# Weight signs from a parametric ReLU, other banks for the first scan units, and an emptied table of due times

## The chip, the cores and the metric

The kernel runs on one core of a Trainium2 chip. A core has five engines with their own instruction queues: TensorE (matrix products, writing to the PSUM memory), VectorE, ScalarE and GpSimd (elementwise work), and SyncE, which here issues all the DMA transfers. Each engine works through its queue in order; semaphores make one wait for another. The metric is the device time of one execution in microseconds.

## The reference

A gated linear recurrence over four batch entries with eight heads gives a sequence of 768 positions per entry; its output, seen as 3072 tokens of 256 values, goes through two feed-forward blocks. Cut to what matters:

```python
def _attn_ref(x, a, B, C):            # x: (4, 8, 768, 32); a: (4, 8, 768); B, C: (4, 8, 768, 16)
    ...
    for c in range(nc):               # chunks of 32 positions
        la = log_a[:, :, sl]
        cum = np.cumsum(la, axis=-1)
        L = np.exp(cum[:, :, :, None] - cum[:, :, None, :]) * causal
        M = np.einsum('bhin,bhjn->bhij', Cc, Bc) * L
        y_intra = np.einsum('bhij,bhjd->bhid', M, xc)
        y_inter = np.einsum('bhin,bhnd->bhid', Cc, state) * np.exp(cum)[:, :, :, None]
        y[:, :, sl] = y_intra + y_inter
        state = decay_full[:, :, None, None] * state + np.sum(Bx, axis=2)

def _moe_ref(x, w_in, w_out):         # w_in: (256, 2048), w_out: (2048, 256)
    h = x @ w_in
    g = np.where(h > 0.0, h, np.exp(np.minimum(h, 0.0)) - 1.0)
    return g @ w_out

def _moe2_ref(x, w_a, w_b, w_out):    # w_a, w_b: (256, 1536), w_out: (1536, 256)
    return ((x @ w_a) * (x @ w_b)) @ w_out
```

The weights arrive as 64-bit floats; the other inputs as 32-bit floats.

## The kernel before, in words

**Tiles and stages.** The 3072 tokens form six tiles of 512. Stage A does the first feed-forward block tile by tile: a tile has eight pairs of 128-wide slices of the hidden layer. For each pair TensorE makes the up product into one of two PSUM buffers of two banks (`up0` for even pairs, `up1` for odd ones), ScalarE and VectorE make the activation, and TensorE accumulates the down product in the two banks `acc0` and `acc1`. Tile 0 uses whole 32-bit operands. Tiles 1 to 5 use operands split into a high and a low part (`hi_`, `lo_` for weights, `gh`, `gl` for activations), three matmuls for one product, twelve per slice. Stage B does the second block: two tiles at a time are taken as a 2 x 2 block product with seven products in place of eight, in 18 groups of two tiles.

**The scan.** The recurrence is cut into 24 units of 128 positions (six chunks of four batch entries). In a unit VectorE scans the decays of its heads (`scan`, L678, in two halves of four heads), TensorE makes the products of B and C (`cbm2` or `cbm`), VectorE multiplies the two (`mask`, L735), GpSimd weights `x` by the last column of the scan (`le`, then `xend`), TensorE makes the output and the addition to the state (`ym`, L770 and L774), and ScalarE copies both out (`state`, `x`). Four units feed one tile; units u0 to u3 feed tile 0. For these four the decays are spread over the partitions by TensorE (`spread`, L654) into two PSUM banks, not loaded by DMA as for the later units. The first pair of tile 0 needs the output of u0 and u1 for its first half of columns, the second pair, in `up1`, that of u2 and u3.

**Weights.** Each weight tile holds 1024 columns as pairs of 32-bit words (`raw`, or `fx` for early ones). `scale` (L523) multiplies the top word, read as a 32-bit float, by 2^-112; `shift` (L528) moves it left by three bits, which drops the sign; `sign` (L531) puts the sign back; `last3` turns the low word into the last three bits; `put` adds them. The result is `m`. Of 17 tiles, eight are made before or in tile 0 (weights of the first block, named m_99, m_100, ... in the listings, in this order: w_in 0, w_out 0, w_in 1, and so on), nine later, for stage B.

**What sets the order.** The whole program is a list of steps with an engine or a choice of two, an estimated cost, the steps it depends on, and a due time. A planner (`Plan.emit`) imitates the engines: it takes, of all ready steps, the one that could start in the earliest window of 0.25 us, and among these the one due first. That fixes each engine's order. `MOVE` shifts the due times of single steps. Where TensorE would wait in the first 50 us by the planner's reckoning, it puts in matmuls on a tile of zeros (`warm`, L419). `Buf.take` gives the steps that must be done before a buffer is written again; `tied` joins two buffers that lie in one PSUM tile.

## Time and profile before

| | |
|---|---|
| time before, median of 3 runs | 616.45 us (616.45 to 617.79) |
| the profiled execution, its own time | 616.54 us |
| its span, first to last instruction | 614.5 us |
| TensorE busy, share of the span | 607.7 us, 99% |
| VectorE busy | 395.9 us, 64% |
| ScalarE busy | 372.1 us, 61% |
| GpSimd busy | 332.0 us, 54% |

Busy time is the sum over an engine's instructions without overlaps. Matmuls are pipelined, so a busy TensorE need not be working on useful products: the zero matmuls count as busy as well. A matmul on 32-bit operands shows as two records in the trace. Idle time is put down to the event that ended it.

### The profile page before, as it was taken

What the parts mean: (1) busy time and instruction counts of PE and PEld (TensorE: products, weight loads), DVE (VectorE), ACT (ScalarE), POOL (GpSimd) and SP (SyncE); (2) the same over time, 40 slices, a digit from 0 to 9 for tenths busy, and PEclk for the clock granted to TensorE, in tenths of its full rate; (3) what the DMA queues carried; (4) which work ended last, traced back from release to release, by engine and by line L of the source; (5) the groups of instructions that cost most, each with busy time, mean ns of one, the idle gap of its engine ahead of it and who ended that gap; (6) DMA issues with size and microseconds to landing.
All of it is one profiled execution on the core that took longest, in us unless ns stands there. A gap on an engine that the chain in (4) does not pass through costs nothing.

```text
span 614.5 us, 9444 instructions
## 1 busy us (share of the span) xinstructions
PE 607.7 (99%) x3627; PEld 481.8 (78%) x3627; DVE 395.9 (64%) x534; ACT 372.1 (61%) x529; POOL 332.0 (54%) x250
## 2 busy tenths in 40 slices
PE   9999999999999999999999999999999999999997
PEld 8875457778778877877888888888888888888885
DVE  7878869788787878868655646756533446433344
ACT  2565767756767766647767655556544556545453
POOL 2423466565556564256445476767655656555542
PEclk9999999999999999999999999999999999999999
DMA  8949633677677736410000000000100000100001
GB/s 236 313 164 306 200 102 126 224 243 248 195 239 271 285 120 201 157 52 0 2 1 1 1 0 1 0 1 1 69 0 2 0 1 0 70 0 1 1 0 68
DMA packets 33404, 59.94 MB, mean 98 GB/s; under 512 B 2736, under 2 KB 13904, under 8 KB 33360
## 3 DMA queue, kind: packets, MB, share of 16 engines
q1 hardware_dynamic: 33360, 59.35, 29.0%
q8 instruction: 28, 0.46, 0.3%
q14 instruction: 16, 0.13, 0.1%
HBM read 47.61 MB, written 11.73 MB: 97 GB/s over the span
## 4 chain that ended last, share of the span: by engine, by line
PE 98%; DVE 0%; ACT 0%; issue 0%; POOL 0%; POOLq 0%
PE acc L857 6%; PE acc L853 6%; PE up L841 6%; PE up L842 6%; PE acc L854 6%; PE up L844 6%; PE up L1186 5%; PE up L1182 5%; PE up L1183 5%; PE up L832 5%; PE acc L832 5%; PE acc L1242 4%; PE acc L1244 4%; PE acc L1243 4%; PE cbank L1242 3%; PE cbank L1244 3%
## 5 line engine op out<-in xcount | busy, mean ns | idle before, releaser
L1271 DVE TENSOR_TENSOR x<-x 128x512 f32<-128x512 f32 x36 | 30.6, 854 | 67.4 <-POOL x L1315 67.0
L940 ACT ACTIVATE e<-up 128x1024 f32<-128x1024 f32 x44 | 45.1, 1026 | 38.5 <-PE up L844 26.2
L1277 POOL TENSOR_TENSOR gl<-x,gh 128x512 fp32r<-128x512 f32 x35 | 48.5, 1387 | 35.4 <-ACT gh L1274 35.2
L961 POOL TENSOR_TENSOR gl<-e,gh 128x1024 fp32r<-128x1024 f32 x20 | 50.9, 2543 | 27.2 <-ACT gh L954 21.9
L1315 POOL TENSOR_TENSOR x<-e,x 128x512 f32<-128x512 f32 x36 | 46.7, 1314 | 33.7 <-ACT e L1254 32.9
L853 PE MATMUL acc<-gh,hi_w_out 128*128 128x512 f32 x160 | 63.6, 397 | 0.0
L854 PE MATMUL acc<-gh,lo_w_out 128*128 128x512 f32 x160 | 62.4, 390 | 0.0
L944 ACT ACTIVATE e<-e,bias 128x1024 f32<-128x1024 f32 x44 | 50.8, 1154 | 0.9
L857 PE MATMUL acc<-gl,hi_w_out 128*128 128x512 f32 x160 | 51.3, 396 | 0.0
L678 DVE TENSOR_TENSOR_SCAN ab<-ab,delta 128x512 f32<-128x512 f32 x36 | 50.0, 1406 | 2.0 <-DMA ab<-a_seg 2.0
L541 POOL TENSOR_TENSOR m<-m,raw 128x1024 int32<-128x1024 int32 x11 | 26.7, 2430 | 25.8 <-DVE m L531 5.5
L841 PE MATMUL up<-xh,hi_w_in 128*128 128x512 f32 x96 | 39.4, 410 | 0.0
L950 DVE SCALAR_TENSOR_TENSOR up<-e,up 128x512 f32<-128x512 f32 x40 | 27.7, 693 | 17.8 <-ACT e L944 17.1
L842 PE MATMUL up<-xh,lo_w_in 128*128 128x512 f32 x96 | 37.5, 390 | 0.0
L1183 PE MATMUL up<-gh,lo_w_out 128*128 128x512 f32 x96 | 37.4, 389 | 0.0
L1182 PE MATMUL up<-gh,hi_w_out 128*128 128x512 f32 x96 | 37.4, 389 | 0.0
L1262 DVE TENSOR_TENSOR p<-acc,p 128x512 f32<-128x512 f32 x36 | 24.2, 688 | 20.3 <-PE acc L1244 18.2
L950 DVE SCALAR_TENSOR_TENSOR e<-e,up 128x512 f32<-128x512 f32 x48 | 30.6, 678 | 10.4 <-ACT e L944 10.4
L1274 ACT CAST gh<-x 128x512 fp32r<-128x512 f32 x36 | 22.4, 624 | 23.6 <-DVE x L1271 23.5
L1262 DVE TENSOR_TENSOR x<-acc,x 128x512 f32<-128x512 f32 x36 | 23.9, 686 | 19.3 <-PE acc L1244 19.2
L1277 POOL TENSOR_TENSOR gl<-p,gh 128x512 fp32r<-128x512 f32 x18 | 23.9, 1325 | 21.2 <-issue 21.2
L853 PEld LDWEIGHTS acc<-gh,hi_w_out 128*128 128x128 f32 x160 | 30.1, 188 | 6.0
(306 smaller groups left out, 1733.1 us busy)
## 6 DMA issues: line engine op xcount, KB each, us to landing
ab<-a_seg SPq DMA_DIRECT2D x18, 512.0 KB
parts<-raw SPq DMA_DIRECT2D x64, 128.0 KB
sm<-parts SPq DMA_DIRECT2D x16, 512.0 KB
p<-in_xb SPq DMA_DIRECT2D x20, 256.0 KB
raw<-in_w_out SPq DMA_DIRECT2D x4, 1024.0 KB
fx<-in_w_out SPq DMA_DIRECT2D x3, 1024.0 KB
out_t<-m SPq DMA_DIRECT2D x12, 256.0 KB
raw<-in_w_in SPq DMA_DIRECT2D x2, 1024.0 KB
```

What stands on the lines that cost most here:

```text
L832: nc.tensor.matmul(ps, w_mm(name, wm, f, c), src, start=start, stop=stop)
L841: nc.tensor.matmul(ps, w_mm(name, whi, f, c), xh[:, c, :], start=(c == 0), stop=False)
L842: nc.tensor.matmul(ps, w_mm(name, wlo, f, c), xh[:, c, :], start=False, stop=False)
L853: nc.tensor.matmul(accs[m], w_mm(name, whi, f, m), gh, start=(f == 0), stop=False)
L854: nc.tensor.matmul(accs[m], w_mm(name, wlo, f, m), gh, start=False, stop=False)
L857: nc.tensor.matmul(accs[m], w_mm(name, whi, f, m), gl, start=False, stop=(f == last))
L944: nc.scalar.activation(gf, gf, AF.Identity, bias=bias[:, 0:1])
L950: nc.vector.scalar_tensor_tensor(u[:, k, :] if on_dve else gf[:, k, :], gf[:, k, :], 0.0, u[:, k, :], op0=ALU.min, op1=ALU.max)
L961: nc.gpsimd.tensor_sub(gl.ap, gf, gh.ap.bitcast(F32))
L1182: nc.tensor.matmul(a4[m].ap, w_mm("w_out2", whi, f, m), gh, start=first, stop=False)
L1183: nc.tensor.matmul(a4[m].ap, w_mm("w_out2", wlo, f, m), gh, start=False, stop=False)
L1277: eng[e].tensor_sub(tap("l" + w), tap(wa), tap("h" + w).bitcast(F32))
```

## The change

**Sign.** `scale` becomes a ScalarE activation, a parametric ReLU with scale 2^-112 and slope 2^32 for negative values. A negative weight so gets 32 added to its exponent, and this bit becomes the sign bit in the shift. `sign` and its step are gone; `put` waits for `shift` instead. `scale` has ScalarE alone now, where it had a choice of ScalarE and VectorE.

**Banks.** u0 to u3 all spread their decays into `acc0` and `acc1`; before, u2 and u3 used the two banks of `up1`. Their products of B and C go to `cbank` and one bank of `up0` (u0, u2), one bank each of `up0` and `up1` (u1), and both banks of `up1` (u3). Banks of one PSUM tile no longer wait for each other (`tied` is gone). The last column `le` of u0 to u3 is copied by ScalarE, no longer by VectorE.

**Planner.** The transfer model allows eight loads in flight at a time and has other constants; the engines' hand-over costs are smaller; zero matmuls are put in for a wait less 0.2 us; `MOVE` is empty. The set-up of the head mask is a step of its own.

The diff, cut to its core:

```diff
-MM = 0.2282
+MM = 0.2272
...
 MOVE = {
-    ("bc", (0, 1, 1)): {"": 7.7, "cast": 5.0},
-    ("bc", (0, 2, 0)): {"": -5.4, "load": 2.3, "rest": -6.3},
...
 }
...
     def take(self):
         old, self.users = self.users, []
-        for b in self.tied:
-            old = old + b.users
         return old
...
-    SYNC = {"PE": 0.27, "ACT": 0.12, "DVE": 0.12, "POOL": 0.12, "SP": 0.0}
-    SAME = {"PE": 0.0, "ACT": 0.06, "DVE": 0.1, "POOL": 0.08, "SP": 0.0}
+    SYNC = {"PE": 0.27, "ACT": 0.12, "DVE": 0.12, "POOL": 0.12, "SP": 0.05}
+    SAME = {"PE": 0.0, "ACT": 0.04, "DVE": 0.06, "POOL": 0.04, "SP": 0.0}
+    LAG = {"PE": 0.0, "ACT": 0.1, "DVE": 0.08, "POOL": 0.04}
...
-                    m = int((start - free["PE"]) * rate / 0.054)
+                    m = int((start - free["PE"] - 0.2) * rate / 0.054)
...
                 for kb in c:
-                    dma = max(dma, end + 1.75) + kb / 250.0
-                    end += 0.45
-                free[e], end = end, dma + 0.6
+                    if len(landed) >= 8:
+                        end = max(end, landed[-8])
+                    dma = max(dma, end + 1.5) + kb / 310.0 + 0.05
+                    landed.append(dma)
+                    end += 0.46
+                free[e], end = end, dma
...
-                free[e] = end
+                free[e] = end - self.LAG[e]
...
-    for i in range(2):
-        cb1[1 + 2 * i].tied, cb1[2 + 2 * i].tied = [cb1[2 + 2 * i]], [cb1[1 + 2 * i]]
...
         def scale(e):
-            if e == "ACT":
-                nc.scalar.mul(m, top.bitcast(F32), 2.0 ** -112)
-            else:
-                nc.vector.tensor_scalar(m, top.bitcast(F32), 2.0 ** -112, None, op0=ALU.mult)
+            nc.scalar.activation(m, top.bitcast(F32), AF.Prelu, scale=2.0 ** -112, alpha=2.0 ** 32)
...
-        def sign(e):
-            nc.vector.scalar_tensor_tensor(mi, top, -0x80000000, mi, op0=ALU.bitwise_and, op1=ALU.bitwise_or)
...
-        i2 = add({"ACT": 1.155, "DVE": 0.75}, scale, i1, mbf.take(), due=due, port=True)
-        i3 = add({"DVE": 0.75}, shift, i2, due=due, port=True)
-        i4 = add({"DVE": 1.3}, sign, i3, due=due, port=True)
+        i2 = add({"ACT": 1.155}, scale, i1, mbf.take(), due=due, port=True)
+        i3 = add({"DVE": 0.7}, shift, i2, due=due, port=True)
...
-            sp = accb if u < 2 else cb1[3:5]
-            cb_ = [[cbb, cb1[1]], [cb1[2], cb1[3]], [cbb, accb[1]], [cbb, cb1[3]]][u]
+            sp = accb
+            cb_ = [[cbb, cb1[1]], [cb1[2], cb1[3]], [cbb, cb1[1]], [cb1[3], cb1[4]]][u]
...
-            i_le = add({"DVE": 0.1} if n == 0 else {"ACT": 0.2}, last_col, i_scan, le.take(), due=due)
+            i_le = add({"ACT": 0.2}, last_col, i_scan, le.take(), due=due)
```

**What moves.** In the listings a number behind a name tells copies of a buffer apart: sm_79 and sm_80 hold B and C of u0 and u1, and of u2 and u3; ab_81, ab_82, f_hi_w_out_94 and f_lo_w_out_95 are the decays of u0 to u3; up_117 and up_118 are `up0` and `up1`.

TensorE, from u1's output (L770, L774) to u2's products of B and C (L719), before:

```order
L770 MATMUL ybank<-ab_82,p_78 32x128 x8
L774 MATMUL ybank<-xe,p_78 32x64 x4
L654 MATMUL up_118<-a_114,delta 128x128 x8
L719 MATMUL cbank<-sm_80 128x128
L719 MATMUL acc_120<-sm_80 128x128
```

TensorE, from u1's output (L667, L671) to u3's products of B and C (L616), in the changed kernel:

```order
L667 MATMUL ybank<-ab_82,p_78 32x128 x8
L671 MATMUL ybank<-xe,p_78 32x64 x4
L551 MATMUL acc_119<-a_114,delta 128x128 x4
L551 MATMUL acc_120<-a_114,delta 128x128 x4
L616 MATMUL up_118<-sm_80 128x128 x8
```

Behind u1's output the spread of u3 follows now, into the accumulator banks; the spread of u2 (L551) and its products stand in the ten rows ahead of it. Between u1's products and its output 42 zero matmuls stood before; there are none now.

VectorE, from the shift of weight m_99 to u3's masks, before:

```order
L528 TENSOR_SCALAR m_99<-m_99 128x1024
L531 SCALAR_TENSOR_TENSOR m_99<-raw_75,m_99 128x1024
L678 SCALAR_TENSOR_TENSOR f_hi_w_out_94<-up_118,delta 128x512 x2
L695 COPY le_67<-f_hi_w_out_94 128x8
L735 TENSOR_TENSOR f_hi_w_out_94<-cbank,f_hi_w_out_94 128x512
L735 TENSOR_TENSOR f_hi_w_out_94<-acc_120,f_hi_w_out_94 128x512
L678 SCALAR_TENSOR_TENSOR f_lo_w_out_95<-up_118,delta 128x512 x2
L695 COPY le_68<-f_lo_w_out_95 128x8
L528 TENSOR_SCALAR m_100<-m_100 128x1024
L531 SCALAR_TENSOR_TENSOR m_100<-fx_92,m_100 128x1024
L735 TENSOR_TENSOR f_lo_w_out_95<-cbank,f_lo_w_out_95 128x512
L735 TENSOR_TENSOR f_lo_w_out_95<-up_118,f_lo_w_out_95 128x512
```

VectorE, the same place in the changed kernel:

```order
L430 TENSOR_SCALAR m_99<-m_99 128x1024
L575 SCALAR_TENSOR_TENSOR f_hi_w_out_94<-acc_119,delta 128x512
L575 SCALAR_TENSOR_TENSOR f_hi_w_out_94<-acc_120,delta 128x512
L575 SCALAR_TENSOR_TENSOR f_lo_w_out_95<-acc_119,delta 128x512
L632 TENSOR_TENSOR f_hi_w_out_94<-cbank,f_hi_w_out_94 128x512
L632 TENSOR_TENSOR f_hi_w_out_94<-up_117,f_hi_w_out_94 128x512
L575 SCALAR_TENSOR_TENSOR f_lo_w_out_95<-acc_120,delta 128x512
L430 TENSOR_SCALAR m_100<-m_100 128x1024
L632 TENSOR_TENSOR f_lo_w_out_95<-up_118,f_lo_w_out_95 128x512 x2
```

Both `sign` (L531) and both `le` (L695) are gone, the shift of m_99 stands directly ahead of u2's scan, and the two halves of u3's scan lie on both sides of u2's masks.

ScalarE, from its first weight operation to u1's copies, before:

```order
L523 ACTIVATE m_99<-raw_75 128x1024
L788 COPY state<-ybank 128x64
L806 COPY x_90<-ybank 128x2x128
L536 ACTIVATE raw_75<-raw_75 128x1024
L788 COPY state<-ybank 128x64
L806 COPY x_90<-ybank 128x2x128
```

ScalarE, the same place in the changed kernel:

```order
L590 COPY le_67<-ab_81 128x8
L427 ACTIVATE m_99<-raw_75 128x1024
L434 ACTIVATE raw_75<-raw_75 128x1024
L685 COPY state<-ybank 128x64
L703 COPY x_90<-ybank 128x2x128
L590 COPY le_68<-ab_82 128x8
```

The last columns of u0 and u1 (L590) are new here, and both weight operations (L427, L434) stand ahead of u0's state and x now.

VectorE, the first odd pair of tile 1, from its activation (L950) on, before:

```order
L950 SCALAR_TENSOR_TENSOR up_118<-e_84,up_118 128x512 x2
L959 TENSOR_TENSOR gl_89<-up_118,gh_86 128x512 x2
L485 TENSOR_TENSOR lo_w_out_944<-m_104,hi_w_out_862 128x1024
L950 SCALAR_TENSOR_TENSOR e_83<-e_83,up_117 128x512 x2
```

VectorE, the first odd pair of tile 1, from its activation (L847) to its residual (L856), in the changed kernel:

```order
L847 SCALAR_TENSOR_TENSOR up_118<-e_84,up_118 128x512 x2
L388 TENSOR_TENSOR lo_w_out_809<-m_102,hi_w_out_740 128x1024
L388 TENSOR_TENSOR lo_w_out_822<-m_104,hi_w_out_796 128x1024
L632 TENSOR_TENSOR ab_81<-cbank,ab_81 128x512
L856 TENSOR_TENSOR gl_89<-up_118,gh_86 128x512 x2
```

Two low parts of weights and a mask now stand between the activation and the residual of this pair; nothing did before.

## Rows read from the trace of the kernel before

**Rows 1.** Busy time by stretch: start, end, length, each engine, clock, DMA.
```profile
core 0: us, PE busy (x) PEld busy (x) DVE busy (x) ACT busy (x) POOL busy (x), PEclk, DMA share, GB/s
0.00:31.00 31.00, 28.63 (x378) 26.11 (x379) 25.44 (x38) 12.90 (x19) 10.28 (x18) 1.00 0.90 275
31.00:600.00 569.00, 569.00 (x3208) 447.71 (x3207) 364.01 (x488) 354.99 (x503) 317.88 (x229) 1.00 0.26 89
400.00:500.00 100.00, 100.00 (x443) 82.81 (x442) 47.33 (x64) 54.65 (x97) 60.64 (x45) 1.00 0.03 11
```

**Rows 2.** Timeline of TensorE to 31 us: start, length, instruction, count, idle before.
```profile
1.06 3.22 PE L419 MATMUL ybank<-zt 128*128 128x128 bf16 x31 [1.06 <-POOL zt L415]
...
18.73 2.05 PE L654 MATMUL up<-a,delta 128*128 128x128 f32 x16 [0.51 <-DVE f_hi_w_out L678]
...
21.40 1.99 PE L832 MATMUL up<-x,m 128*128 128x256 f32 x8
...
27.51 0.64 PE L770 MATMUL ybank<-f_lo_w_out,f_lo_w_out 128*32 128x128 f32 x16
...
29.07 1.50 PE L419 MATMUL ybank<-zt 128*128 128x128 bf16 x24 [0.81 <-ACT x L806]
...
30.41 1.95 PE L832 MATMUL up<-x,m 128*128 128x256 f32 x8
```

**Rows 3.** Chain that ended last, in order of time: start, length, instructions.
```profile
10.10 1.09 PE up L719 x16
...
30.57 1.78 PE up L832 x8
```

**Rows 4.** Timeline of VectorE, units u0 to u3.
```profile
5.26 2.34 DVE L678 TENSOR_TENSOR_SCAN ab<-acc,delta 128x512 f32<-128x512 f32 x2 [0.28 <-PE acc L654]
...
11.76 1.29 DVE L735 TENSOR_TENSOR ab<-up,ab 128x512 f32<-128x512 f32 x2
12.97 0.68 DVE L528 TENSOR_SCALAR m<-m 128x1024 int32<-128x1024 int32 x1
13.68 1.22 DVE L531 SCALAR_TENSOR_TENSOR m<-raw,m 128x1024 int32<-128x1024 int32 x1
16.34 2.34 DVE L678 TENSOR_TENSOR_SCAN f_hi_w_out<-up,delta 128x512 f32<-128x512 f32 x2 [1.43 <-PE up L654]
...
20.82 2.34 DVE L678 TENSOR_TENSOR_SCAN f_lo_w_out<-up,delta 128x512 f32<-128x512 f32 x2 [0.47 <-PE up L654]
```

**Rows 5.** Timeline of ScalarE to 30 us.
```profile
0.80 1.28 ACT L423 ACT_TABLE_LOAD   x1 [0.80 <-PEq L1487]
...
9.23 1.18 ACT L523 ACTIVATE m<-raw 128x1024 f32<-128x1024 f32 x1 [6.93 <-DMA raw<-in_w_in]
...
17.64 1.13 ACT L523 ACTIVATE m<-fx 128x1024 f32<-128x1024 f32 x1 [2.76 <-DMA fx<-in_w_out]
...
28.65 0.37 ACT L806 COPY x<-ybank 128x256 f32<-128x256 f32 x1
```

**Rows 6.** Instructions by line and shape: count, busy us, mean ns, idle before.
```profile
L944 ACT ACTIVATE e<-e,bias 128x1024 f32<-128x1024 f32 x44 | 50.8, 1154 | 0.9
...
L940 ACT ACTIVATE e<-up 128x1024 f32<-128x1024 f32 x44 | 45.1, 1026 | 38.5 <-PE up L844 26.2 <-PE up L832 7.9 <-POOL p L756 1.7
...
L950 DVE SCALAR_TENSOR_TENSOR up<-e,up 128x512 f32<-128x512 f32 x40 | 27.7, 693 | 17.8 <-ACT e L944 17.1
...
L959 DVE TENSOR_TENSOR gl<-up,gh 128x512 fp32r<-128x512 f32 x40 | 25.7, 683 | 7.5 <-ACT gh L954 7.5
...
L954 ACT CAST gh<-up 128x1024 fp32r<-128x1024 f32 x20 | 20.3, 1014 | 12.8 <-DVE up L950 12.7
...
L531 DVE SCALAR_TENSOR_TENSOR m<-raw,m 128x1024 int32<-128x1024 int32 x12 | 14.6, 1219 | 0.1
...
L419 PE MATMUL ybank<-zt 128*128 128x128 bf16 x135 | 9.9, 237 | 1.9 <-POOL zt L415 1.1 <-ACT x L806 0.8
```

**Rows 7.** Waits of SyncE's queue to 90 us: total, times, longest.
```profile
SPq L514 <- POOL m L541: 4.3, 1, 4.3
```

More of the change, by code (lines that the diff above doesn't have):

```diff
@@ L64 @@
-    ("group", 4): {"": 0.8, "hi": -2.2, "lo": 1.7, "mm3": 2.5},
-    ("group", 5): {"": -8.2, "cp": 0.2, "dn_h": 0.5},
-    ("late", 0): {"comb": 2.6},
-    ("late", 1): {"": 0.1},
-    ("late", 3): {"": -10.3},
-    ("late", 4): {"high": 3.0},
-    ("late", 5): {"": 3.5, "high": 9.5},
-    ("late", 6): {"": 8.5, "high": -13.9},
-    ("late", 7): {"": -14.4, "comb": 10.6},
-    ("late", 8): {"": 0.3, "high": -6.8},
-    ("pair", (0, 0)): {"": -7.7},
-    ("pair", (0, 5)): {"": -2.6},
-    ("pair", (0, 7)): {"": 2.8},
@@ L100 @@
-    ("pair", (5, 0)): {"": 5.7},
-    ("pair", (5, 1)): {"up_a": -3.1},
-    ("pair", (5, 3)): {"up_a": -7.0},
-    ("pair", (5, 4)): {"up_a": 0.1},
-    ("pair", (5, 5)): {"": 5.8},
-    ("pair", (5, 6)): {"": 4.7, "up_a": -6.5},
-    ("pair", (5, 7)): {"": -0.7, "dn_h": 3.4},
-    ("split", ("w_in", 0)): {"high": -20, "rest": -2.9},
-    ("split", ("w_in", 1)): {"": -1.8, "high": -2.8},
-    ("split", ("w_in", 3)): {"": 6.1, "high": 3.2},
-    ("split", ("w_out", 0)): {"": 1.5},
-    ("split", ("w_out", 1)): {"": -8.2},
@@ L112 @@
-    ("unit", 0): {"": 8.5, "ld0": -15.4, "ld_x": -9.9, "mask": -5.0},
-    ("unit", 1): {"ld0": 7.0, "ld_x": 13.0},
-    ("unit", 10): {"ld_a": -20, "st_bd": -5.0},
-    ("unit", 11): {"scan": 6.0, "st_up": 8.5},
-    ("unit", 12): {"": -12.6, "ld_a": 5.9},
-    ("unit", 13): {"": -7.7, "<lambda>": 3.6, "scan": -4.3},
-    ("unit", 14): {"": -0.6, "ld_sm": 4.0, "scan": -2.6, "st_bd": -4.2},
-    ("unit", 15): {"": -3.8, "<lambda>": 11.8, "cbm": 6.9, "ld_a": 18.7, "scan": 5.9},
-    ("unit", 16): {"": -8.1, "st_bd": -7.0},
@@ L121 @@
-    ("unit", 17): {"": -9.6, "last_col": 17.8},
-    ("unit", 18): {"scan": 6.9, "st_bd": 10.0},
-    ("unit", 19): {"": 6.4, "cbm": 8.3, "st_bd": -16.1},
-    ("unit", 2): {"ld0": 12.2},
-    ("unit", 20): {"": -4.8, "<lambda>": -18.3, "ld_db": -6.6, "ld_x": -2.5, "scan": 9.0},
-    ("unit", 21): {"": 5.1, "ld_x": -4.6, "mask": 8.5, "scan": -4.0},
-    ("unit", 22): {"<lambda>": 14.0, "cbm": -2.1, "ld_a": -9.9, "scan": 1.5, "x_lo": 15.3},
-    ("unit", 23): {"mask": 7.9, "scan": 4.2, "st_bd": -12.9},
@@ L129 @@
-    ("unit", 3): {"ld_x": 12.1},
-    ("unit", 5): {"last_col": 16.9, "x_hi": 20},
-    ("unit", 6): {"": 2.8, "<lambda>": 6.4, "ld_a": -5.0, "ld_x": 2.7},
-    ("unit", 7): {"": 3.0, "<lambda>": -1.2, "ld_a": -1.9, "ld_x": -3.6, "st_bd": -0.4},
-    ("unit", 8): {"": 10.9, "ld_a": -7.3, "scan": -4.6, "st_up": 6.9, "x_lo": 3.9, "xend": -3.1},
-    ("unit", 9): {"": 2.0, "ld_a": -3.0, "ld_sm": 2.5},
-    ("w", ("w_in", 1)): {"shift": -19.7},
-    ("w", ("w_in", 2)): {"put": 8.6},
-    ("w", ("w_in", 3)): {"": 4.1, "scale": 7.8},
@@ L138 @@
-    ("w", ("w_out", 1)): {"put": -20, "sign": -11.6},
-    ("w", ("w_out", 2)): {"sign": -6.5},
-    ("w", ("w_out", 3)): {"load": -16.2, "sign": 4.2},
-    ("wb", ("w_a", 0)): {"": -0.2, "last3": 7.5, "load": 0.2},
-    ("wb", ("w_a", 1)): {"": -11.5},
-    ("wb", ("w_a", 2)): {"": 12.0, "shift": -2.6, "sign": -2.6},
-    ("wb", ("w_b", 0)): {"": -8.4, "scale": -20, "sign": -6.0},
-    ("wb", ("w_b", 1)): {"": -8.8, "last3": 18.2, "shift": 18.2},
-    ("wb", ("w_b", 2)): {"": 10.0, "last3": -3.0, "load": 7.0, "sign": 15.3},
@@ L147 @@
-    ("wb", ("w_out2", 0)): {"": 4.1, "sign": -9.5},
-    ("wb", ("w_out2", 1)): {"sign": 6.5},
-    ("wb", ("w_out2", 2)): {"last3": 13.0, "load": 16.4, "put": 10.3, "scale": 12.6, "shift": -0.1, "sign": -3.4},
-    ("xset", 1): {"": -11.8, "x_h": -13.3, "x_l": 0.9},
 }
@@ L214, in emit @@
         port, dma, done = 0.0, 0.0, 0
+        landed = []
         self.log = []
@@ L753, in st_bd @@
                     hmask.rearrange("p (q e) -> p q e", e=2).unsqueeze(3).to_broadcast([P, 4, 2, D]))
-            i_sbd = add({"POOL": 0.82}, st_bd, i_state[b], sbd.take(), i_ones, due=due, port=True)
+            i_sbd = add({"POOL": 0.82}, st_bd, i_state[b], sbd.take(), i_heads, due=due, port=True)
             i_cd = add({"POOL": 0.72}, lambda e: nc.gpsimd.tensor_mul(cd, cd, dbt), i_p, i_db, due=due, port=True)
```

45 lines of the change are left out of this document (8 added, 37 removed), and 4 rows, old and new, of the table MOVE.

## The prediction

> **What bounds the kernel now.** I read the busy times by stretch first [rows 1]. From 31 to 600 us TensorE is busy for 569.00 of 569.00 us at a granted clock of 1.00, which is the 2.4 GHz level; no other engine passes two thirds there (VectorE 364 us, ScalarE 355 us). Nothing that the change takes off VectorE can shorten that stretch. In the first 31 us TensorE counts 28.63 us as busy, but its timeline [rows 2] shows that part of this is padding: L419, a matmul on a tile of zeros, which runs 135 times in all [rows 6], 31 of them at the very start and 24 just ahead of 30.41. Its real waits are small, 1.06, 0.51 and 0.81 us [rows 2], because the padding stands where waits would be. So time can be won only in front of the second pair of tile 0, the last work that has padding ahead of it; it starts at 30.41 [rows 2]. The VectorE timeline [rows 4] shows what that start waits for: one chain of scan, mask, scan, mask over the units u0 to u3, with the preparation of the first weights in between.
>
> **The change, part by part.**
>
> *Sign.* Per weight tile of 1024 columns one VectorE instruction of 1219 ns goes [rows 6], 17 of them (twelve in that row, five on the early buffers), some 21 us. In the saturated stretch this is worth nothing, since TensorE covers it. In the first 31 us one sign (1.22 us, at 13.68 [rows 4]) stands directly ahead of u2's scan and a second one ahead of u3's masks; these two are on the chain. On ScalarE the multiplication of weight m0 (1.18 us [rows 5]) becomes a parametric ReLU of the same shape, and the one weight of 17 that VectorE scaled goes there too. The trace has no such ReLU: the nearest rows are ScalarE's exponential (1026 ns) and its identity with a bias (1154 ns) on as many columns [rows 6]. I take 1.15 us, no change; at the other bound, twice that, the first weight holds u0's state and u1's last column 1.15 us longer, all of it on the chain. A second function table is not loaded: the trace has one table load, 1.28 us at 0.80 [rows 5], and the changed order has one too.
>
> *Banks.* Before, u2 and u3 spread their decays into the two banks of `up1`, and u3's spread had to wait for u2's scan; VectorE sat idle 1.43 us at 16.34 and 0.47 us at 20.82 for these two spreads [rows 4]. Now all four units use the two accumulator banks, and u2's spread stands on TensorE ahead of u1's output matmuls instead of behind them (listing on TensorE). It needs only u1's scan, so it is done by about 12.9, before VectorE asks for it.
>
> *Last column.* The copy `le` of u0 to u3 leaves VectorE for ScalarE. For u1 it queues there behind both operations of weight m0 and the copies of u0 (listing on ScalarE), which start when the weight lands, at 9.23 [rows 5]: 9.23 + 1.18 + 1.13 for the second operation, of the same shape, + about 0.5 for the copies gives 12.05. Before, u1's masks started at 11.76 [rows 4]; I charge the change 0.35 us.
>
> *Walk through the start.* TensorE has 19 zero matmuls first, not 31; at 3.22/31 = 0.104 us [rows 2] that is 1.25 us less, but u0's scan gains only the 0.28 us that it waited [rows 4]. Then on VectorE: u1's masks 12.1 to 13.4 (1.29), one shift (0.68) to 14.05, u2's scan (2.34) to 16.4, where it ended at 18.7. Next come half of u3's scan, u2's masks, the other half, one shift and u3's masks (listing on VectorE): 1.2 + 1.3 + 1.2 + 0.7 + 1.3 = 5.7, so 22.05. Needed on the way is weight m1, whose load landed by 17.64 [rows 5]; its two ScalarE operations end at 19.9, ahead of the shift at 20.1. On TensorE: u2's output 19.0 to 19.7; the first pair of tile 0, whose two halves stand together now, 2 x 1.78 [rows 3] to 23.25; u3's output to 24.0. ScalarE does the first exponential (1.03), then u3's copies, to 24.9; before, the copy of `x` ended at 28.65 + 0.37 = 29.02 [rows 5]. Fifteen zero matmuls at 1.50/24 = 0.0625 us [rows 2] make 0.95: the second pair starts at 25.9. Against 30.41 that is **4.5 us earlier**. The work left behind this point is the same in both kernels, and TensorE had no wait in it [rows 1].
>
> *Loads.* SyncE issues in order. The load of the third w_in tile now stands ahead of u5's decays and its rows of B and C. It waits for GpSimd to finish with weight m1, as it did before (4.3 us [rows 7]), and now u5's loads wait behind it, until about 24 by the walk. u5's scan follows u4's masks, which come after the second pair and the first down matmuls, near 35; the loads have some 5 us of cover. Without it, u5's masks and its output on TensorE would be late by as much.
>
> *Emptied table.* Due times decide between steps that are ready together; they shift the interleaving in the saturated stretch. The tightest place I find is the odd pairs of tiles 1 to 5: VectorE makes their residual out of a bank of `up1`, and the pair after next needs this bank. The chain is 1.03 + 1.15 + 2 x 0.69 + 1.01 + 2 x 0.68 = 5.9 us [rows 6], and TensorE does three groups of 12 matmuls meanwhile, 36 x 100/443 = 8.1 us [rows 1], which leaves 2.2 us less hand-overs. What else VectorE does between the last two steps eats this: in all 20 odd pairs 27 instructions before, 31 after, at most three in one pair in either kernel (second listing on VectorE: the first pair, one of the worst). The stalls that this could cause were absent before. I take 0 for it, and 0.4 us per odd pair as the other bound.
>
> **Sum.** The profiled execution took 616.54 us, 614.5 of it span and 2.0 around it, 0.09 above the median of 616.45. 616.5 - 4.5 = **612.0 us**.
>
> **The rivals.**
>
> *A, the forecast:* 610.5 to 613.5. For it: each piece gained is a wait or an instruction in rows 2 and 4 that has no place in the new order.
>
> *B, the start is gained in part.* Weight operations stand at the head of ScalarE's and VectorE's queues more often now. A load that lands 2 us later, or a ReLU 1.15 us slower, goes through to the masks. Price 1 to 4 us: 613 to 616.
>
> *C, the odd pairs stall (slower).* If the residuals come late by 0.4 us beyond the room in each of 20 odd pairs, and the first group stage loses 2 us to the same cause, that is 10 us: 612 + 10 = 622. It decides against the change from 0.32 us per pair (6.4 us in all). Against it: the new order alternates up and down matmuls strictly, pair by pair, which the old one did not, and 31 instructions are hardly more than 27.
>
> *D, the clock at the start.* 94 of the 135 zero matmuls are gone. The trace shows 0.104 us for each of the first 31 and 0.0625 for the last 24 [rows 2], near the ratio of 1.2 to 2.4 GHz, although the granted clock reads 1.00 in the whole stretch [rows 1]; the later rows all hold the faster pace. If with fewer zero matmuls TensorE ran at the lower level from 5 to 19 us, three spreads of 2.0 [rows 2], four score groups of 1.1 [rows 3] and two outputs of about 0.7, 11.8 us, would take 23.6: 12 us later, less 2 us of slack, less the 4.5 gained: 616.5 + 5.5 = 622. The Trainium skill, "TensorE: Matmul & The Clock Gate", Part 1 ("The HAM clock gate"), says that the throttled state is the default and that activity releases it; the first row agrees, and by that rule alone the padding was no waste. Against D: in my walk TensorE does real matmuls in over four fifths of that time.
>
> *E, more than forecast.* From 3 us on TensorE's real work ahead of the second pair is four spreads, four score groups, four outputs and the first pair, 8.0 + 4.4 + 2.8 + 3.6 = 18.8 us. If it never waited, the second pair would start at 21.8, 8.6 us earlier: 608.
>
> **How the numbers follow.** A 0.57, B 0.22, C 0.10, D 0.06, E 0.05. The likeliest is A: 612.0. A measurement of this kernel tells 0.3% from no change, 1.85 us: faster is below 614.6, slower above 618.3. Faster: A, E and half of B, 0.73. Same: the rest of B and a weak C, 0.14. Slower: the rest of C and D, 0.13. The range from 610.2 to 617.5 leaves out most of E and the bulk of C and D, under 2 in 10.
>
> **What would show it.** Right: the second pair of tile 0 (now L729, `up1`) starts near 26; VectorE's scan of u2 starts near 14 and shows no wait for TensorE; TensorE's busy share stays at 100% from there to the end. Wrong by B: that start lies between 27 and 30, with a wait for a DMA or for ScalarE ahead of a mask or a shift. Wrong by C: waits of TensorE for VectorE at the up matmuls after 80 us. Wrong by D: spreads that take 4 us instead of 2. The whole is wrong if the time moves without that start moving.

## The result: the start came as forecast, the time went the other way

The changed kernel takes 626.58 us (median of four runs, 622.83 to 627.16), the kernel before beside it 616.6 us. The ratio is 1.0145, with a 95% interval of 1.0103 to 1.0186: slower by nine to ten microseconds, where 4.5 less were forecast. The profiled execution took 627.16 us and has a span of 625.5 us; before it was 614.5 us.

First the stretches of [rows 1], and three more, in the changed kernel. The columns are the busy time of each engine, then the granted clock of TensorE as a share of 2.4 GHz.

```profile
core 0: us, PE busy (x) PEld busy (x) DVE busy (x) ACT busy (x) POOL busy (x), PEclk, DMA share, GB/s
0.00:31.00 31.00, 29.13 (x306) 26.25 (x307) 24.73 (x34) 14.03 (x24) 10.63 (x18) 1.00 0.91 291
31.00:600.00 569.00, 559.12 (x3141) 438.29 (x3140) 340.07 (x467) 352.08 (x497) 301.88 (x221) 0.99 0.26 88
400.00:500.00 100.00, 100.00 (x443) 82.81 (x442) 48.14 (x68) 54.45 (x96) 58.79 (x43) 1.00 0.03 11
...
98.80:105.60 6.80, 5.80 (x18) 4.31 (x19) 2.55 (x4) 2.87 (x3) 2.37 (x1) 0.50 0.27 103
180.70:184.10 3.40, 3.21 (x11) 2.63 (x11) 2.53 (x5) 2.39 (x4) 3.37 (x4) 0.50 0.34 106
96.00:99.80 3.80, 0.24 (x2) 0.00 (x1) 3.43 (x4) 3.50 (x5) 1.25 (x2) 0.86 0.69 198
```

Before, TensorE was busy for all of 31 to 600 us. Now 9.88 us are missing there, in one of the stretches TensorE does next to nothing, and in two the clock is at 0.50, the 1.2 GHz level. From 400 to 500 us nothing changed (443 matmuls, as before). VectorE has 24 us less work in the second row (21.5 us less in the whole execution, 395.9 to 374.4, about what the removed signs promised), and it bought nothing.

The start, TensorE's timeline, to be read against [rows 2]:

```profile
1.06 2.21 PE L319 MATMUL ybank<-zt 128*128 128x128 bf16 x19 [1.06 <-POOL zt L315]
3.16 3.66 PE L551 MATMUL acc<-a,delta 128*128 128x128 f32 x16
...
24.92 1.00 PE L319 MATMUL ybank<-zt 128*128 128x128 bf16 x15 [0.81 <-ACT x L703]
25.75 3.67 PE L729 MATMUL up<-x,m 128*128 128x256 f32 x16
```

The second pair starts at 25.75, forecast 25.9, before 30.41: 4.66 us were won. Who took them back is in the list of TensorE's waits (total, times, longest):

```profile
PE cbank L629 <- DVE ab L632: 4.9, 1, 4.9
PE cbank L629 <- DMA sm<-parts: 3.6, 1, 3.6
PE ybank L663 <- issue: 1.3, 1, 1.3
PE ybank L319 <- POOL zt L315: 1.1, 1, 1.1
PE ybank L319 <- ACT x L703: 0.8, 1, 0.8
PE up L1083 <- DVE gl L1174: 0.6, 1, 0.6
```

The fourth and fifth were there before [rows 2]. The other four are new, 10.5 us together; the smallest, 0.6 us, lies near the end of stage B. The three large ones belong to the scan units u6, u8 and u15, and each goes back to a DMA that landed after an engine had come to the step that needs it:

**56.6 us, 1.35 us.** SyncE issues the load of weight w_out 2 at 46.96, behind parts stores. ScalarE has its scale next and sits until the load is there; VectorE's next step is that weight's shift; u6's masks stand behind the shift. So a weight that no product needs yet holds u6's output on TensorE. The list names no releaser for this wait ("issue"); the chain is read from the order of the queues and from the times, the second mask ending at 57.81 and TensorE going on at 57.91:

```profile
54.74 1.15 ACT L427 ACTIVATE m<-fx 128x1024 f32<-128x1024 f32 x1 [4.74 <-DMA fx<-in_w_out]
```
```profile
55.92 0.69 DVE L430 TENSOR_SCALAR m<-m 128x1024 int32<-128x1024 int32 x1 [4.65 <-ACT m L427]
56.53 0.68 DVE L632 TENSOR_TENSOR ab<-cbank,ab 128x512 f32<-128x512 f32 x1
57.13 0.68 DVE L632 TENSOR_TENSOR ab<-ybank,ab 128x512 f32<-128x512 f32 x1
```

**96.2 us, 3.56 us.** The eight parts stores ahead of it take SyncE from 87.39 to 93.24; the load of `sm` for u8 and u9, which reads what the stores write, goes out at 96.18, just as TensorE comes to u8's products, at 96.24 (SyncE's queue, then TensorE):

```profile
87.39 5.85 SPq L484 DMA_DIRECT2D parts<-raw  x8
...
96.18 0.90 SPq L523 DMA_DIRECT2D sm<-parts  x2
```
```profile
99.80 0.61 PE L629 MATMUL cbank<-sm 128*128 128x128 bf16 x4 [3.56 <-DMA sm<-parts]
```

Before, SyncE issued this load later still, at 103.59; but u8's products stood further back on TensorE, and ran at 108.41 without a wait:

```profile
103.59 0.90 SPq L626 DMA_DIRECT2D sm<-parts  x2
...
108.41 0.40 PE L732 MATMUL cbank<-sm 128*128 128x128 bf16 x4
```

**176.0 us, 4.94 us.** The list names a mask of VectorE. The mask waited 6.30 us for ScalarE's last column, and ScalarE had been waiting for the load of weight w_out2 0, issued at 170.46 behind sixteen parts stores, with the last column behind that weight in its queue. That weight is for stage B, more than 100 us later.

```profile
176.48 1.12 ACT L427 ACTIVATE m<-raw 128x1024 f32<-128x1024 f32 x1 [4.89 <-DMA raw<-in_w_out]
...
179.91 0.20 ACT L590 COPY le<-ab 128x8 f32<-128x8 f32 x1
```
```profile
180.15 0.69 DVE L632 TENSOR_TENSOR ab<-cbank,ab 128x512 f32<-128x512 f32 x1 [6.30 <-ACT le L590]
```

**The clock.** In the second and third of these waits the granted clock falls to 0.50 and stays there for some microseconds after TensorE has work again. At half speed, half of the busy time is lost: 5.80/2 + 3.21/2 = 4.5 us.

The sum: - 4.66 + 10.5 + 4.5 = + 10.3 us, against a difference of the spans of 625.5 - 614.5 = 11.0. About 0.7 us stay unassigned.

### The profile page after: what moved, and what is told of

Read it like the earlier page. It is cut to its first block, busy times and chain, and to the rows that moved or that the text cites. A ratio compares the mean times of both kernels' runs of the same rounds, so it can differ in the third digit from the quotient of the medians.

```text
span 625.5 us, 9248 instructions
## 1 busy us (share of the span) xinstructions
PE 608.7 (97%) x3533; PEld 480.8 (77%) x3533; DVE 374.4 (60%) x515; ACT 375.6 (60%) x536; POOL 321.6 (51%) x245
## 4 chain that ended last, share of the span: by engine, by line
PE 87%; DMA 5%; ACT 3%; DVE 1%; issue 1%; SPq 1%; POOL 1%; POOLq 0%; ACTq 0%; DVEq 0%
PE acc L754 6%; PE acc L750 6%; PE acc L751 6%; PE up L738 6%; PE up L739 5%; PE up L741 5%; PE up L1083 5%; PE up L1080 5%; PE up L1079 5%; PE acc L1140 4%; PE acc L1141 4%; PE acc L1139 4%; PE ybank L1140 3%; PE cbank L1140 3%; PE ybank L1141 3%; PE ybank L1139 3%
## 5 line engine op out<-in xcount | busy, mean ns | idle before, releaser
L858 POOL TENSOR_TENSOR gl<-e,gh 128x1024 fp32r<-128x1024 f32 x20 | 49.0, 2448 | 62.0 <-ACT gh L851 57.4
L1168 DVE TENSOR_TENSOR x<-x 128x512 f32<-128x512 f32 x36 | 29.0, 807 | 74.2 <-POOL x L1212 73.7
L847 DVE SCALAR_TENSOR_TENSOR up<-e,up 128x512 f32<-128x512 f32 x40 | 27.8, 695 | 26.5 <-ACT e L841 25.7
L847 DVE SCALAR_TENSOR_TENSOR e<-e,up 128x512 f32<-128x512 f32 x48 | 30.7, 681 | 18.9 <-ACT e L841 18.9
L738 PE MATMUL up<-xh,hi_w_in 128*128 128x512 f32 x96 | 41.2, 430 | 0.0
L632 DVE TENSOR_TENSOR ab<-cbank,ab 128x512 f32<-128x512 f32 x35 | 24.0, 687 | 20.2 <-PE cbank L629 11.9
L751 PEld LDWEIGHTS acc<-gh,lo_w_out 128*128 128x128 f32 x160 | 30.4, 190 | 6.3
```

What stands on the lines that cost most here:

```text
L738: nc.tensor.matmul(ps, w_mm(name, whi, f, c), xh[:, c, :], start=(c == 0), stop=False)
L751: nc.tensor.matmul(accs[m], w_mm(name, wlo, f, m), gh, start=False, stop=False)
L847: nc.vector.scalar_tensor_tensor(u[:, k, :] if on_dve else gf[:, k, :], gf[:, k, :], 0.0, u[:, k, :], op0=ALU.min, op1=ALU.max)
```

## Experiments

All ratios are to the kernel before, run beside them on the same chip. Theory T: the emptied table is the cause. Theory M: the new transfer model is too optimistic. Theory C: the clock is a cost of its own.

**1. The clock alone.** Zero matmuls go ahead of the two products that wait; they only fill the wait.

```diff
             def cbm(e, g=g):
+                warm({(8, 0): 56, (15, 1): 79}.get((u, g), 0))
```

> The changed kernel with matmuls on the tile of zeros put in front of the two products that wait, 56 ahead of u8's first and 79 ahead of u15's second, about as long as each wait (0.0625 us each). Nothing else moves. Theory C (the slow matmuls behind the waits are the granted clock, which fell because TensorE was idle): the matmuls behind them keep 0.227 us, the granted clock stays at 1.00, 626.6 - 2.9 - 1.5 = 622.2. Rival (the slow pace comes from what follows, such as operands that come late): 626.6, clock or pace as before.

Measured: 623.10 us, 1.0098 (1.0082 to 1.0115); the span 621.2 us, 4.3 less than the changed kernel's. The same stretches as above:

```profile
96.00:100.00 4.00, 4.00 (x64) 3.69 (x64) 2.94 (x4) 2.82 (x4) 1.43 (x2) 1.00 0.71 266
100.00:106.00 6.00, 6.00 (x44) 4.60 (x46) 3.70 (x6) 3.21 (x3) 1.28 (x1) 1.00 0.23 87
```

The clock stays at 1.00 and from 100 to 106 us 44 matmul records fit where there were 21. u8's products come at 99.42, hardly earlier: the wait is the same, only the price behind it is gone. Theory C holds, 4.3 us of 4.4 expected by the spans (by the medians 3.5 us, and the intervals of the two kernels overlap).

**2. The table back.** The changed kernel with the old table.

```diff
 MOVE = {
+    ("bc", (0, 1, 1)): {"": 7.7, "cast": 5.0},
+    ("bc", (0, 2, 0)): {"": -5.4, "load": 2.3, "rest": -6.3},
...
 }
```

> The changed kernel with the table of the kernel before put back; transfer model and constants stay new. Theory T (the emptied table made the waits): the waits of TensorE ahead of u8's products (3.56 us) and of u15's (4.94 us) go, with the slow stretches behind them, and the earlier start remains: 616.5 - 4.7 = 611.8, say 611 to 614. Rival M (the new transfer model is too optimistic, whatever the table): the planner still puts u8's products at 96 us by its own reckoning, so a wait of some 3 us for the load sm<-parts stays and the clock falls behind it: 618 to 626.

Measured: 622.71 us, 1.0093 (1.0073 to 1.0113). This is in rival M's range. The wait of 3.56 us ahead of u8's products is down to 0.3 us, but others came, the longest of the same kind, for the same tensor, at another unit:

```profile
190.86 0.40 PE L730 MATMUL cbank<-sm 128*128 128x128 bf16 x4 [3.12 <-DMA sm<-parts]
```

T alone falls: with the table back, most of the loss stays.

**3. The table alone.** The kernel before with `MOVE` empty and nothing else.

> The kernel before with its table emptied and nothing else. Theory T: the same kind of waits appears as in the changed kernel, 10 to 15 us: 626 to 631. Rival M: the old transfer model, which takes 0.6 us more for a landing and 250 bytes per ns, places steps behind their loads without a table too: 616 to 619, and TensorE has no wait over 2 us after 31 us.

Measured: 624.67 us, 1.0121 (1.0106 to 1.0136), between the two forecasts. So M alone falls as well: with the old model too the table was worth over 1%. But its longest wait is 1.8 us, half of the changed kernel's 3.56 or less, and it has one slow stretch in place of two (0.50 from 174.4 to 177.8). The waits behind the start, that stretch and a second pair at 32.04 in place of 30.41 come to 7.6 of the 9.2 us by which the span grew (614.5 to 623.7). The largest entry of its list:

```profile
PE acc L756 <- POOL gl L860: 2.4, 2, 1.8
```

**4. The new code in the old planner**, without a table (first) and with the old one (second). Both have the changed kernel's sign, banks and last column. Transfer model and hand-over costs go back; a few small things of the new planner stay, among them the estimate `MM` and the 0.2 us taken off each wait that is filled with zero matmuls.

```diff
-    SYNC = {"PE": 0.27, "ACT": 0.12, "DVE": 0.12, "POOL": 0.12, "SP": 0.05}
-    SAME = {"PE": 0.0, "ACT": 0.04, "DVE": 0.06, "POOL": 0.04, "SP": 0.0}
+    SYNC = {"PE": 0.27, "ACT": 0.12, "DVE": 0.12, "POOL": 0.12, "SP": 0.0}
+    SAME = {"PE": 0.0, "ACT": 0.06, "DVE": 0.1, "POOL": 0.08, "SP": 0.0}
...
-                    if len(landed) >= 8:
-                        end = max(end, landed[-8])
-                    dma = max(dma, end + 1.5) + kb / 310.0 + 0.05
-                    landed.append(dma)
-                    end += 0.46
-                free[e], end = end, dma
+                    dma = max(dma, end + 1.75) + kb / 250.0
+                    end += 0.45
+                free[e], end = end, dma + 0.6
...
-                free[e] = end - self.LAG[e]
+                free[e] = end
```

> The new code (sign, banks, last column) with the planner of before, its transfer model and hand-over costs, and an empty table. Theory M: few waits over 2 us, 612 to 616. Theory T: as the kernel before with an empty table (624.67), less the start's 4 us: 619 to 622, with one or two waits of 2 to 4 us and a stretch of lower clock between 150 and 200 us.

> The new code with planner and table of before, so that sign, banks and last column are all that changed. If a table carries over to other code: start 4 us earlier and no waits, 612 to 613. If a table is worth its gain only for the code that it was fitted to: waits come back though the table is there, 616 to 622.

Measured: 621.33 us, 1.0075 (1.0058 to 1.0092) without the table; 615.51 us, 0.9974 (0.9963 to 0.9984) with it. The first is in theory T's range. The second is faster than the kernel before. Its second pair starts at 25.39, and its waits after the start are these three of the list:

```profile
PE up L836 <- DVE e L945: 1.6, 1, 1.6
PE up L1177 <- ACT gh L1269: 1.3, 2, 1.1
...
PE ybank L761 <- POOL f_lo_w_out L751: 0.3, 1, 0.3
```

Together with experiment 2 this makes a square for the new code, as ratios: old planner and table 0.9974, old planner alone 1.0075, table alone 1.0093, neither 1.0145. Each of the two is worth 0.5 to 1.2%, whether the other is there or not; only the smallest of the four differences, 0.5% for the table with the new planner, is not clear of noise, since the intervals of its two kernels overlap. Transfer model and hand-over costs went back together here; experiment 5 changes the loads alone. Whether a table carries over to other code is answered in between: about 3 of the 5 us won at the start were lost again.

**5. Better loads, no table.** Three forms: constants nearer to the measured landings (first), any step that uses a load reckoned 2 us later (second), a time of its own for each size (third, with 0.1 in place of 0.05 us from a landing to the step that uses it).

```diff
-                    dma = max(dma, end + 1.5) + kb / 310.0 + 0.05
-                    landed.append(dma)
-                    end += 0.46
-                free[e], end = end, dma
+                    dma = max(dma, end + 1.50) + kb / 290.0 + 0.05
+                    landed.append(dma + 0.60)
+                    end += 0.63 if kb <= 128 else 0.46
+                free[e], end = end, dma + 0.60
```
```diff
+                    slack = 2.0 if ea == "SP" and end > 30.0 else 0.0
-                    end += (self.SYNC[ea] if ea != e else self.SAME[e]) + (pad if ea != e else 0.0)
+                    end += (self.SYNC[ea] if ea != e else self.SAME[e]) + (pad if ea != e else 0.0) + slack
```
```diff
+    def took(self, i, kb):
+        part = self.parts[i][0]
+        if kb == 1024 and part[1][0] in ("w_out", "w_out2"):
+            return 3.9
+        return {64: 0.37, 96: 0.4, 128: 0.8, 256: 0.7, 512: 1.4, 1024: 2.7}[kb]
...
-                    dma = max(dma, end + 1.5) + kb / 310.0 + 0.05
+                    dma = max(dma, end + 2.25) + 1.05 * self.took(i, kb)
                     landed.append(dma)
-                    end += 0.46
+                    end += 0.62 if kb <= 128 else 0.44
```

> The changed kernel, table empty, with a transfer model made after its own trace: 290 bytes per ns in place of 310, 0.6 us more until a landing is seen (the trace: 2.6 us for a 128 KB store alone, the model 2.0), 0.63 us per issue of small transfers in place of 0.46. Theory M (the steps stand ahead of their loads because the planner believes loads too early): no wait of TensorE over 2 us, granted clock at 1.00 to 600 us, start as in the changed kernel: 613 to 616. Theory T (without its table the planner makes such waits with any model): waits of 3 to 5 us and a lower clock stay somewhere between 90 and 200 us, 619 to 625.

> The changed kernel, table empty, its own transfer model, but after 30 us every step that waits for a load is taken to be free 2 us later, so that the planner puts it further back: u8's products at 111 in its reckoning, 95 in the changed kernel's. Theory M: the wait at u8 is gone and none over 2 us is left, 612 to 616. Rival: the loads themselves follow the late steps, since buffers come free later, and the waits only move: 618 to 625.

> The same transfer model as the run before, with an empty table. What it has over that run is what the table is worth once the loads are reckoned rightly. If the model alone does it: 611 to 613. If both are needed: 614 to 618, with waits of 1 to 3 us between 90 and 210 us.

Measured: 617.87 us, 1.0019 (0.9997 to 1.0040); 619.55 us, 1.0037 (1.0022 to 1.0052); 617.13 us, 0.9996 (0.9982 to 1.0011). The first lies between its two forecasts, the second in the rival's range, the third where table and model are both needed. So a transfer model that gives a load its time is worth 1.1 to 1.5% with an empty table, 7 to 9 us. None came to the 612 of the start's gain. What waits stay go through other engines, as in the third form at 147.8 us, where VectorE's scan waited 2.51 us for its load of decays, the activation stood behind the scan, and TensorE waited 3.1 us for the activation, after which the clock was at 0.52 from 152.0 to 155.4:

```profile
PE up L744 <- DVE e L853: 3.1, 1, 3.1
```

**6. Two entries by hand.** u8's products and weight w_out2 0 put later, the rest as in the changed kernel.

```diff
 MOVE = {
+    ("unit", 8): {"cbm": 34.0},
+    ("wb", ("w_out2", 0)): {"": 25.0},
 }
```

> The changed kernel with two entries in its empty table: u8's products 34 us later in due time, weight w_out2 0 25 us later. Both theories: the two waits (3.56 and 4.94 us) and the slow stretches behind them (about 2.9 and 1.5 us at a pace of 0.427 in place of 0.227 us per matmul) go, 626.6 - 12.9 = 613.7; the wait of 1.35 us at 56.6 stays. Rival: a wait only moves to the next late load, 618 to 626.

Measured: 622.37 us, 1.0080 (1.0057 to 1.0104), so the rival: the wait at u8 is gone and weight w_out2 0 no longer holds u15, but three waits came, of 3.1, 1.8 and 1.4 us. The longest stands at the same product of u15 where the changed kernel had 4.94 us, and goes back to another load, for which ScalarE waits with the last column behind it:

```profile
178.70 0.38 PE L631 MATMUL cbank<-sm 128*128 128x128 bf16 x4 [3.13 <-DVE ab L634]
```
```profile
177.20 0.62 ACT L478 CAST raw<-raw 128x512 bf16<-128x512 f32 x1 [5.30 <-DMA raw<-in_ct]
```

**7. The parts of the code, one at a time**, in the kernel before with its planner and table: the sign alone (first), then banks and last column alone (second; `tied` goes with the banks).

```diff
-            if e == "ACT":
-                nc.scalar.mul(m, top.bitcast(F32), 2.0 ** -112)
-            else:
-                nc.vector.tensor_scalar(m, top.bitcast(F32), 2.0 ** -112, None, op0=ALU.mult)
+            nc.scalar.activation(m, top.bitcast(F32), AF.Prelu, scale=2.0 ** -112, alpha=2.0 ** 32)
...
-        i2 = add({"ACT": 1.155, "DVE": 0.75}, scale, i1, mbf.take(), due=due, port=True)
+        i2 = add({"ACT": 1.155}, scale, i1, mbf.take(), due=due, port=True)
...
-        i4 = add({"DVE": 1.3}, sign, i3, due=due, port=True)
...
```
```diff
-        for b in self.tied:
-            old = old + b.users
...
-            sp = accb if u < 2 else cb1[3:5]
-            cb_ = [[cbb, cb1[1]], [cb1[2], cb1[3]], [cbb, accb[1]], [cbb, cb1[3]]][u]
+            sp = accb
+            cb_ = [[cbb, cb1[1]], [cb1[2], cb1[3]], [cbb, cb1[1]], [cb1[3], cb1[4]]][u]
...
-            i_le = add({"DVE": 0.1} if n == 0 else {"ACT": 0.2}, last_col, i_scan, le.take(), due=due)
+            i_le = add({"ACT": 0.2}, last_col, i_scan, le.take(), due=due)
```

> The kernel before with the sign made by the parametric ReLU and nothing else; its table and planner stay. If the sign has its worth by itself: start 0.5 us earlier, u3's spread waits for u2's scan as before, 616 us. If a table holds only for the code that it was fitted to: the order moves, waits of 1 to 3 us come in between 90 and 210 us, 618 to 621.

> The kernel before with the other banks for u0 to u3 and the last column on ScalarE, and nothing else; its table, planner and sign stay. If the banks carry the start: second pair 2 us earlier, near 28.4; time 614.6 if no waits come in. If a table holds only for the code that it was fitted to: waits, 618 to 625, with the start gained all the same.

Measured: 623.68 us, 1.0104 (1.0088 to 1.0120), and 623.97 us, 1.0112 (1.0099 to 1.0125). The second pair of each, sign first:

```profile
31.18 1.95 PE L824 MATMUL up<-x,m 128*128 128x256 f32 x8
```
```profile
28.17 2.16 PE L828 MATMUL up<-x,m 128*128 128x256 f32 x9
```

The sign alone brings the start no nearer (0.8 us later than before), the banks alone 2.2 us, both together 4.7 to 5.0. These starts are not quite alike: in the two executions the first spread took 2.66 and 3.00 us, 2.00 before, behind the same 31 zero matmuls, and u0's scan began at 6.14 and 6.40, 5.26 before. Counted from there the sign alone brings 0.1 us and the banks alone 3.4. Why the sign brings nothing by itself shows in u2's scan, which starts at 17.22 in that kernel: the 1.22 us that the sign frees ahead of it go into a longer wait for u2's spread, 2.70 us where it was 1.43 [rows 4], because that spread still stands behind u1's output.

And each alone, under a table that was fitted to other code, lost 6 to 9 us behind the start: with the sign to waits of 3.6 us in the list and a slow stretch (0.50 from 155.9 to 159.3), with the banks to waits of 7 us in the list. The rest of it is not assigned.

**8. A table fitted to this code.** The third model of experiment 5 and a new table of 105 entries, chosen so that the order, gone through with the measured durations and landings, leaves TensorE no waits. The second such table was also to leave room for small delays and to have no gaps in the first 30 us.

```diff
 MOVE = {
+    ('bc', (0, 2, 0)): {"": 2.8},
+    ('group', 0): {"": 7.0, "ad": 4.2, "dn_l": -4.6},
...
 }
```

> The changed kernel with a transfer model made after the measured landings (each size has its own time: 0.8 us for 128 KB, 1.4 for 512, 2.7 for 1024 or 3.9 for w_out, 2.25 us from issue to the first landing) and with a new table of 105 entries, fitted to this code and this model. Theory (the edits to the code are worth their 4.7 us, and all that was lost was lost to the order): second pair near 25.8, no wait of TensorE over 1 us after 31 us, granted clock at 1.00 to 600 us: 616.5 - 4.7 = 611.8, or 609.5 to 612 as far as the kernel before had waits of its own. Rival (what the changed kernel lost lies in the code: a ScalarE and a VectorE queue that hold more): waits of 2 us and more stay, 615 to 619.

> The changed kernel with the transfer model after its landings and a second table of 105 entries, fitted so that small delays on the other engines do no harm and TensorE has no gap in the first 30 us. Theory (the code's 4.7 us can be kept whole): second pair at 25.8, granted clock at 1.00 from 5 us to the last few us, no wait over 0.5 us after 31 us: 616.5 - 4.7 = 611.8, 611 to 613. Rival (some 2 us of waits come with the code whatever the order): 614 to 616, as the first refitted table gave (614.29).

Measured: 614.29 us, 0.9954 (0.9943 to 0.9966), and 613.70 us, 0.9940 (0.9928 to 0.9952): both beat both kernels, and both lie between the theory's range and the rival's. The first has its second pair only at 28.37 (u4's products stand ahead of it) and a slow stretch at the start, which is experiment 9. In the second the second pair starts at 26.09, and 2.0 us of waits are left after it, where the changed kernel had 10.5. That is the amount that the rival named; that they come with the code in any order is not shown:

```profile
26.09 3.67 PE L806 MATMUL up<-x,m 128*128 128x256 f32 x16
```
```profile
PE up L815 <- DVE gl L933: 0.9, 2, 0.4
PE acc L831 <- POOL gl L935: 0.8, 1, 0.8
...
PE cbank L706 <- DVE ab L709: 0.3, 1, 0.3
```

**9. The clock at the start.** In the first of these two kernels the clock was at 0.50 for 3.4 us in the start itself, after two short gaps of TensorE, 0.49 us in the 4.7 us ahead. Twelve zero matmuls go ahead of the products that stood behind the gaps.

```diff
             def cbm2(e):
+                warm({1: 4, 2: 8}.get(u, 0))
```

> The kernel with the first refitted table, and twelve zero matmuls more: four ahead of u1's products of B and C, eight ahead of u2's, where TensorE had been idle 0.22 and 0.33 us. Its trace showed the granted clock at 0.50 from 14.7 to 18.1 us. Theory (the clock fell for lack of work at the start, the mechanism of rival D): it stays at 1.00, u0 to u3 are done 1.7 us earlier, 614.29 - 1.7 = 612.6. Rival (the clock there falls whatever TensorE does, or the units wait for VectorE anyway): the stretch at 0.50 stays, or goes without a gain, 614.3.

The stretch without the zeros and with them:

```profile
10.00:14.70 4.70, 4.21 (x42) 3.66 (x43) 3.45 (x5) 2.56 (x5) 0.62 (x1) 1.00 0.67 178
14.70:18.10 3.40, 3.40 (x35) 2.94 (x35) 2.56 (x3) 0.51 (x3) 2.60 (x2) 0.50 1.00 337
```
```profile
10.00:14.70 4.70, 4.70 (x57) 4.18 (x53) 3.38 (x5) 2.63 (x5) 0.62 (x1) 1.00 0.75 171
14.70:18.10 3.40, 3.27 (x44) 2.79 (x45) 2.93 (x5) 0.59 (x3) 2.29 (x2) 1.00 0.87 290
```

The slow stretch is gone, the second pair comes 1.0 us earlier (28.37 to 27.34, both behind u4's products) and the span is 1.3 us shorter (613.6 to 612.3). The medians say less: 614.13 us, 0.9950 (0.9938 to 0.9963), the intervals lie over each other. So the clock can fall at the start, and with the zeros it did not in the profiled execution. In most executions of the kernel without them it seems not to fall: their mean granted clock is 0.996 in two of six, those that took longest (615.30 and 615.32 us), and 0.998 to 0.999 in the other four (613.21 to 614.67).

**10. Code or fitting?** The same model and a table fitted in the same way (136 entries) for the code of the kernel before.

> The code of the kernel before (its sign, its banks) with the transfer model and the hand-over costs of the refitted kernels, and a table of 136 entries fitted to it in the same way. Theory (the code carries the gain): the second pair stays near 30 and the time is 616 to 618, some 3 us over the second refitted table's 613.70. Rival (the fitting carries it, the new code adds nothing): 613 to 614.5.

Measured: 618.35 us, 1.0021 (1.0012 to 1.0030). It has no more than 0.4 us of waits after the start, and its second pair starts near 31.8:

```profile
31.79 1.51 PE L816 MATMUL up<-x,m 128*128 128x256 f32 x6
```

The time is just above the theory's range. The fitting alone gains nothing; with the new code it is 4.65 us less (618.35 to 613.70), the second pair 5.7 us earlier, some 1.6 us of that lost to waits. The code carries the gain. The order found for the old code is no better than the one it had, so the 4.65 is a difference of two tries, not of two best orders; against the kernel before with its own table (617.3 us beside it) the new code gains 3.6 us.

## Why the prediction was wrong

**The start: right.** The walk came to 25.9, it was 25.75; u2's scan was forecast for 14.05 and ran at 13.96 with no wait for TensorE:

```profile
13.96 2.33 DVE L575 TENSOR_TENSOR_SCAN f_hi_w_out<-acc,delta 128x512 f32<-128x512 f32 x2
```

*Sign*: the parametric ReLU takes 1156 ns, as the multiplication did (1153), and there was one table load. *Banks* held: u2's spread was done at 13.65, before VectorE came to u2's scan; without the sign this was worth 3.4 us (experiment 7).

Two errors made one right number, which is luck. *Walk* assumed 2.00 us for the first spread; it took 3.66, at about half the pace, and u0's masks began 0.44 us later than before. *Last column* charged 0.35 us because the copy of u1 would queue behind both operations of weight m0. It did not: those and u0's copies were done at 11.58, and ScalarE then waited 0.34 us for u1's scan, which was late because of the first spread. So u1's masks began at 12.16, where 12.1 was forecast, for another reason than the one given:

```profile
11.92 0.20 ACT L590 COPY le<-ab 128x8 f32<-128x8 f32 x1 [0.34 <-DVE ab L575]
```

**The step that failed: *Emptied table*, taken at 0**, and with it the sentence in *Walk* that the work left behind is the same and "TensorE had no wait in it". The new transfer model and hand-over costs have no term in the sum at all, so they too were taken at 0, without a reason. In place of 0 the runs showed 10.5 us of waits and 4.5 us of slow clock. That there was no wait [rows 1] was a property of one order and of the loads' times in it, not of the work. Three things were missed in it:

- I looked for cover at one place, the odd pairs, where VectorE's chain is tight. No up matmul of the first block waited in the changed kernel, so rival C's mechanism did not occur there (in other orders up matmuls did wait for VectorE, 1.6 us in experiment 4). The scan units' loads and stores, which the change moved most, were checked for u5 alone (*Loads*, and u5 was indeed not late).
- The diff itself showed what to fear. The new model gives a load of 512 KB 1.5 + 512/310 + 0.05 = 3.2 us, the old one 1.75 + 512/250 + 0.6 = 4.4; the trace has 3.6 from issue to use at u8. Both reckon some 0.46 us for issuing a store; the trace has 0.57 (median of 64), and 5.85/8 = 0.73 with the gaps between them. A planner that believes loads early puts the steps that use them early, and an engine that works in order then waits with everything behind it.
- A regular order was taken as evidence for a smooth one. Strict alternation says who comes after whom, not when a load lands.

The size of this step: no table in place of one, 0.5% with the new planner (1.0093 to 1.0145, not clear of noise) and 1.0% with the old (0.9974 to 1.0075); the new planner in place of the old, 0.7% without and 1.2% with the table. Together 1.7%, 10.6 us, of the 14.6 between the forecast of 612.0 and 626.58. The other 3.5 to 4 us the new code lost with the old planner and table as well (615.51 in experiment 4, 3.2 us of waits): even there the work left behind the start was not without a wait.

**Rival D: right mechanism, mostly another place.** At the start only the first of the four spreads was slow, and that cost 0.44 us at u0's masks. The granted clock fell in the waits, and that cost 4.5 us by the rows, 4.3 by experiment 1, on top of the waits themselves. Rival B has a late load in it, but only at the start; no rival had one behind it, so the range ended at 617.5, nine below the time. The Trainium skill, "TensorE: Matmul & The Clock Gate", Part 1 ("The HAM clock gate"), says that the throttled state is the default and that activity releases it; the trace agrees, at the start and in the middle: zero matmuls in place of idle time kept the clock at 1.00 in experiments 1 and 9.

**The gain was real.** 616.5 - 4.5 = 612.0 was the forecast for this code with an order as good as the old one; the best order found has 613.70, with 2.0 us of waits left.

## What to carry to other kernels

An order without waits belongs to the durations and landings that it was fitted to: when the planner's model or its table changes, look at each DMA that an in-order engine waits for, and at what is queued behind that wait, before counting the gain. A wait of TensorE costs more than its length if the clock falls in it (here 4.5 us on top of 8.5); zero matmuls that fill the wait kept the clock and did not make the waiting product later (99.42 in place of 99.80). A gain at the start reaches the end whole only if the order behind it is fitted again.
